# The zeros ahead of the experts' regions, written during the tenth unit of attention

## The chip, the cores and the metric

The kernel runs on one core of one Trainium2 chip. The metric is the time of the device for one execution, in microseconds (us); the median of the runs is compared.

## What is computed

Three stages follow each other. Attention is computed for 8 batches, 8 heads, 576 positions and 32 memory slots. Its output, 4608 rows of 512 columns, goes through a mixture of 8 experts in which each row uses one expert, and then through a feed-forward network with a hidden width of 2048.

```python
def reference(**kwargs):
    ...
    attn_out = _attn_ref(**attn_kwargs)
    x = np.ascontiguousarray(attn_out.transpose(0, 2, 1, 3)).reshape(B * S, H * D)
    x = _moe_ref(x=x, **moe_kwargs)       # e = argmax of logits; out = gate * relu(x w1[e]) w2[e]
    return _moe2_ref(x=x, **moe2_kwargs)  # softplus(x w_in) w_out
```

## The kernel before

**Attention and routing** (`attention_and_routing`). The 4608 rows are 18 units (`u`) of two tiles of 128 rows. A unit goes through `scores` (matmuls, then maximum, exponential and sum, down to the weights `an`), `transp` (TensorE turns `an`, ScalarE copies it to `aT`), `values` (the matmuls `px`, copied to `xrow`, and the logits `lg`), `route` (the expert of each row) and `rank` (the place of each row in its expert's region). Units 0 to 15 are routed in pairs, the last two alone. `rank` ends with indirect DMAs on GpSimd's queue that write the rows into the DRAM buffer `xs`, which has one region for each expert: 512 rows ahead of it (`PAD`) and then room for 4608 rows. The rows ahead of a region are read when a slot is not full, so they have to hold zeros. `pad` writes them for one expert from the tile `zero`, a transfer of 1056 KB on SyncE's queue; there are eight.

**The first slot.** After unit 10 (`CHOICE`) the counts so far are known. `choose(0, ...)` picks the expert with most rows and a start row into `few` (columns 0 to 2, `pick[0]`). `fetch` makes SyncE load the two values into registers (L468, L469), read 256 rows of `xs` into `raw0` (L51), and load that expert's weights: four tiles of `w1` (buffers `k`) and four of `w2` (buffers `j`), 512 KB each (L102), with the gates `ig0` between them (L473). `chosen` is this slot's computation, spread over the last units by `STEPS`: VectorE turns `raw0` into `xt` (L486), 32 matmuls in full precision make the hidden rows `ph` (L491; the profile counts 64, since each is two instructions), ScalarE and VectorE make `h` from them (L125, L126) and split the tiles of `w2` in two parts (L58, L61), and 48 matmuls make `py` (L67 to L69).

**The second choice** follows the last `rank`: `choose(1, ...)` writes `pick[1]` (L455 to L464). VectorE then builds the table of all further slots (`listed`, L601 to L643).

**The further slots** (`experts`). SyncE loads the start row of the second choice (`head(1, SP, ...)`, L746, a TENSOR_LOAD of `few`) and reads two quarters of 512 rows of `xs` into `raw`; ScalarE's queue reads the other two quarters. VectorE turns `raw` into `xt` (L675), ScalarE and VectorE split it to `hl`, and TensorE starts the slot with the matmuls `ph<-hl,k` (L67 to L69). From there the slots follow each other without a wait, and the last network after them.

**What sets the order.** Every engine runs its instructions in the order of the built program, SyncE its transfers too: an instruction that waits holds all that stand behind it on its engine. In the attention part a planner makes that order: it places an instruction by the time at which it holds its inputs to be ready, so that code written later can stand earlier. A transfer that reads `xs` at a register's row is taken to depend on all writes to `xs` that the code has ahead of it. `once` takes a write out of this against the groups in `apart`: after `fetch` the writes to `xs` are declared apart from its reads ("full"), ahead of it they are not.

Of the kernel before, what the change touches and what calls it, by code (L numbers as in the profile page):

```python
# [25 lines left out]
E, F = 8, 1024  # L26
# [10 lines left out]
TAB = TABU + MAXS  # L37
STEPS = {14: 4, 15: 2, 16: 2, 17: 1}
CHOICE = 10
PADS = range(11, 15)  # L40
PAD = UNIT
RG = PAD + NT
ROW = 528
# [28 lines left out]
def pad(eng, xs, zero, e):  # L72

    return eng.dma_start(xs[e * RG:e * RG + PAD].rearrange("(p a) c -> p a c", p=P),
                         zero.unsqueeze(1).to_broadcast([P, PAD // P, ROW]))
# [101 lines left out]
def attention_and_routing(tc, env):  # L177
    nc = tc.nc
    V, A, G, PE, SP = nc.vector, nc.scalar, nc.gpsimd, nc.tensor, nc.sync
    qT, kv, phi, mid, wg, mbias, w1, w2 = (env[n] for n in ("qT", "kv", "phi", "mid", "wg", "mbias", "w1", "w2"))  # L180
    xs, table, nslots, pick, ig0, ps_y, K, Q, J = (
        env[n] for n in ("xs", "table", "nslots", "pick", "ig0", "ps_y", "K", "Q", "J"))

    with ExitStack() as st:
# [37 lines left out]
        zero = c.tile([P, ROW], F32, name="zero")  # L222
# [20 lines left out]
        def load(b):  # L243
            p0 = 9 * (b // 2)
            lo, hi = (0, 5) if b % 2 == 0 else (5, 9)
            o = b % 2 * 64
            phs[b] = pht[b % 3]
            SP.dma_start(phs[b][:, :, o:o + S], phi[:, b * S:(b + 1) * S].rearrange("(g p) s -> p g s", p=P))
            for t in range(p0 + lo, p0 + hi):
                SP.dma_start(kvt[t % 12], kv[t * P:(t + 1) * P])  # L250
            qs[b] = qst[b % 3]
            SP.dma_start(qs[b], qT[:, b * S:(b + 1) * S].rearrange("(g p) s -> p g s", p=P))
# [97 lines left out]
        def scores(u):  # L350
            ps = ps_s.tile([P, 2, H * M], F32, name="ps", tag="s")
            for k in range(2):
                for p in range(4):
                    for hf in range(2):
                        n = 4 * u + 2 * k + hf
                        b, o = n // 9, (n % 9) * 64
                        PE.matmul(ps[64 * hf:64 * hf + 64, k, 64 * p:64 * p + 64],
                                  qs[b][:, p, o:o + 64],
                                  kvT[b][:, p // 2, 0, 64 * (p % 2):64 * (p % 2) + 64],
                                  start=True, stop=True)  # L360
            s3 = ps.rearrange("p k (h m) -> p (k h) m", m=M)
            mx = sm.tile([P, 2 * H], F32, name="smx", tag="smx")
            V.tensor_reduce(mx, s3, axis=AX, op=ALU.max)
            sc = wk.tile([P, 2 * H, M], F32, name="sc", tag="sc", bufs=3)
            V.tensor_tensor(sc, s3, mx.unsqueeze(2).to_broadcast([P, 2 * H, M]), ALU.subtract)
            A.activation(sc, sc, AF.Exp, scale=0.125)
            ss = sm.tile([P, 2 * H], F32, name="ss", tag="ss")
            V.tensor_reduce(ss, sc, axis=AX, op=ALU.add)
            V.tensor_scalar(ss, ss, 1e-9, None, op0=ALU.add)
            V.reciprocal(ss, ss)  # L370
            an = wk.tile([P, 2 * H, M], F32, name="an", tag="an", bufs=3)
            for k in range(2):
                hs = slice(k * H, (k + 1) * H)
                (V if u >= UNITS - LATE else G).tensor_tensor(an[:, hs], sc[:, hs], ss[:, hs].unsqueeze(2).to_broadcast([P, H, M]), ALU.mult)
            at[u] = an

        def transp(u):
            an = at[u].rearrange("p (j h) m -> p j (h m)", j=4)
            pt = ps_t.tile([P, 4, P], F32, name="pat", tag="t")
            for j in range(4):  # L380
                PE.transpose(pt[:, j, :], an[:, j, :], ident)
            aT = wk.tile([P, 4, P], F32, name="aT", tag="aT", bufs=3)
            A.activation(aT, pt, AF.Copy)
            at[u] = aT

        def values(u, k):
            aT = at[u]
            gi = group[u]
            if u == units[gi][0] and k == 0:
                logit[gi] = sm.tile([P, 2 * len(units[gi]), E], F32, name="lg", tag="lg")  # L390
            lg, xr = logit[gi], xrow[gi % 3]
            W = 2 * D + E
            px = ps_y.tile([P, 2, 512], F32, name="px", tag="y")
            t = 2 * u + k
            halves = [(0, P)] if 2 * t // 9 == (2 * t + 1) // 9 else [(0, 64), (64, 64)]
            for g in range(2):
                for o, n in halves:
                    b = (2 * t + o // 64) // 9
                    for r in (0, 1):
                        PE.matmul(px[o:o + n, r, g * W:(g + 1) * W],  # L400
                                  aT[64 * r:64 * r + 64, 2 * k + g, o:o + n],
                                  vz[b][64 * r:64 * r + 64, g, 2 * D:], start=True, stop=True)
            i = 2 * (u - units[gi][0]) + k
            pw = px[:, :, 0:2 * W].rearrange("p r (g c) -> p r g c", g=2)
            A.activation(xr[:, i, 0:DM].rearrange("p (g r c) -> p r g c", g=2, r=2), pw[:, :, :, 0:2 * D], AF.Copy)
            V.tensor_reduce(lg[:, i, :], pw[:, :, :, 2 * D:].rearrange("p r g e -> p e r g"),
                            axis=mybir.AxisListType.XY, op=ALU.add)
# [44 lines left out]
        def choose(i, rows):  # L452

            n, d, m = cnt
            V.tensor_tensor(n, rows, past[i], ALU.subtract)  # L455
            V.tensor_reduce(most[:, 0:1], n, axis=AX, op=ALU.max)
            V.scalar_tensor_tensor(d, n, most[:, 0:1], desc[0:1], op0=ALU.is_equal, op1=ALU.mult)
            V.tensor_reduce(most[:, 1:2], d, axis=AX, op=ALU.max)
            V.tensor_scalar(pick[i][:, 0:1], most[:, 1:2], -1.0, float(E), op0=ALU.mult, op1=ALU.add)
            V.scalar_tensor_tensor(m, d, most[:, 1:2], past[i], op0=ALU.is_equal, op1=ALU.mult)  # L460
            with nc.allow_low_precision(reason="whole numbers below 2**24"):
                V.tensor_reduce(pick[i][:, 1:2], m, axis=AX, op=ALU.max)
            V.tensor_scalar(d, d, most[:, 1:2], float(UNIT if i else SLOT), op0=ALU.is_equal, op1=ALU.mult)
            V.tensor_tensor(past[i + 1], past[i], d, ALU.add)  # L464

        def fetch():
            W.tiles()
            x0 = SP.value_load(pick[0][:, 1:2], min_val=0, max_val=E * RG - SLOT)  # L468
            e = SP.value_load(pick[0][:, 0:1], min_val=0, max_val=E - 1)  # L469
            read = rows_in(nc, SP, raw0, xs[ds(x0, SLOT)], SLOT)  # L470
            for i in range(4):
                W.load(0, i, e)
            read.append(SP.dma_start(ig0, xs[ds(x0, SLOT), DM:DM + 2].rearrange("(t p) c -> p t c", p=P)))  # L473
            full(tc, *read)
            apart.append("full")
            for i in range(4):
                W.load(1, i, e)
# [23 lines left out]
        def once(w):  # L501

            for group in apart:
                tc.declare_no_dep(w.ins, group=group, reason="disjoint rows")
            tc.add_to_no_dep_group("xs", w.ins)
            return w
# [27 lines left out]
        def point(i):  # L534
            if i in points:
                f, b = points[i]
                f(b)
# [15 lines left out]
        for u in range(UNITS):  # L553
            if u == 0:
                load(2)
            point(4 * u)
            if u + 2 < UNITS:
                scores(u + 2)
            if u in (0, 2, 5, 7, 9):
                load(3 + (0, 2, 5, 7, 9).index(u))  # L560
            point(4 * u + 1)
            values(u, 0)
            point(4 * u + 2)
            if u + 1 < UNITS:
                transp(u + 1)
            values(u, 1)
            if u and u - 1 == units[group[u - 1]][-1]:
                rank(group[u - 1])
                if u == CHOICE:
                    choose(0, base[(group[u - 1] + 1) % 2][0:1])  # L570
                    fetch()
            if u == units[group[u]][-1]:
                route(group[u])
            point(4 * u + 3)
            if u == CHOICE:
                steps = chosen()
            if u in PADS:
                for e in range(2 * (u - PADS[0]), 2 * (u - PADS[0]) + 2):
                    once(pad(SP, xs, zero, e))
            for i in range(STEPS.get(u, 0)):  # L580
                next(steps)
        rank(len(units) - 1)
# [410 lines left out]
```

## Time and profile before

| | us |
|---|---|
| median of 3 runs | 1412.92 |
| lowest and highest of them | 1411.44, 1417.55 |
| profiled execution, time of the device | 1422.22 |
| profiled execution, span | 1420.2 |

The span runs from the first instruction to the last. Of its 1420.2 us TensorE (PE) is busy in 1370.2. Attention, routing and the first slot take the first 182 us, the further slots go on to about 609 us, and the last network ends the span. Times in the rows below are counted from the start of the span. The granted clock of TensorE is given as a share of 2.4 GHz: 0.50 is 1.2 GHz. A duration of a matmul in the profile includes its way through the array, so matmuls that follow each other overlap: 16 of L491 stand in 3.70 us, though each lasts 0.38.

### The profile page before, as it was taken

The page shows a single profiled execution, that of the slowest core. Times are in us where ns is not written, and L with a number is a line of the kernel's source. Part 1 is how long each engine was busy: PE and PEld are TensorE (multiplying, and loading weights), DVE is VectorE, ACT ScalarE, POOL GpSimd, SP SyncE. Part 2 cuts the span into 40 slices and gives each one's busy share as a digit, 9 for nine tenths or more (in the row PEclk, how much of TensorE's full clock was granted, in tenths as well). Part 3 has the DMA queues.
Part 4 walks back from the last instruction along what each step waited for, and adds up shares of the span by engine and source line. Part 5 has one row for each costly group of instructions (what it writes and reads, how often), then busy time and mean ns, then how long its engine had stood idle before and what let it go on. Part 6 is the DMA issues. An engine that isn't in the chain of part 4 may idle for free.

```text
span 1420.2 us, 19794 instructions
## 1 busy us (share of the span) xinstructions
PE 1370.2 (96%) x7312; PEld 1100.9 (78%) x7312; DVE 922.5 (65%) x1699; ACT 674.6 (48%) x1193; POOL 256.9 (18%) x267
## 2 busy tenths in 40 slices
PE   7997989999999999889999999999999999999997
PEld 5775758878888888668888888888888888888885
DVE  4665857777877775769665756657566575665553
ACT  3554435444443445356544545445454454544443
POOL 1343314333434334300100101001010010100101
PEclk8889989999999999999999999999999999999998
DMA  9975984445334566244010200202001020000000
GB/s 357 402 285 202 374 240 102 104 113 140 95 99 127 170 213 182 89 143 133 23 38 0 60 1 23 38 0 60 1 23 38 0 60 1 23 8 1 30 1 30
DMA packets 94338, 143.03 MB, mean 101 GB/s; under 512 B 16160, under 2 KB 54048, under 8 KB 94240
## 3 DMA queue, kind: packets, MB, share of 16 engines
q1 hardware_dynamic: 86320, 120.94, 28.5%
q0 software_dynamic: 5760, 19.17, 3.5%
q10 hardware_dynamic: 2160, 1.63, 0.4%
q8 instruction: 58, 0.95, 0.3%
q14 instruction: 40, 0.33, 0.1%
HBM read 122.28 MB, written 44.62 MB: 118 GB/s over the span
## 4 chain that ended last, share of the span: by engine, by line
PE 50%; issue 6%; POOL 0%; DMA 0%; ACT 0%; DVE 0%; POOLq 0%; SPq 0%
PE po L67 8%; PE po L69 8%; PE po L68 8%; PE ph L67 8%; PE ph L69 8%; PE ph L68 8%; POOL out L928 0%; DMA s<-wsc 0%; POOLq L989 0%; ACT u L908 0%; DVE g L914 0%; DVE c L913 0%; ACT u L909 0%; ACT g L910 0%; ACT k L58 0%
## 5 line engine op out<-in xcount | busy, mean ns | idle before, releaser
L67 PE MATMUL ph<-hl,k 128*128 128x512 f32 (+1 forms) x536 | 204.3, 381 | 8.2 <-ACT hl L58 5.4
L68 PE MATMUL ph<-hl,k 128*128 128x512 f32 (+1 forms) x536 | 204.3, 381 | 0.0
L58 ACT ACTIVATE gh<-g 128x512 fp32r<-128x512 f32 x144 | 91.0, 632 | 228.3 <-DVE g L915 228.0
L912 DVE TENSOR_SCALAR c<-u 128x512 f32<-128x512 f32 x144 | 61.5, 427 | 194.7 <-ACT u L909 185.2
L928 POOL DMA_INDIRECT out<-ob,ids x36 | 41.3, 1147 | 767.9 <-ACT ob L927 661.7
L69 PE MATMUL ph<-hl,k 128*128 128x512 f32 (+1 forms) x456 | 173.1, 380 | 0.0
L61 DVE TENSOR_TENSOR gl<-g,gh 128x512 fp32r<-128x512 f32 x144 | 99.2, 689 | 84.7 <-ACT gh L58 83.7
L908 ACT ACTIVATE u<-ph 128x512 f32<-128x512 f32 x144 | 86.1, 598 | 133.0 <-PE ph L69 128.1
L67 PE MATMUL py<-q,h 128*128 128x512 f32 x304 | 121.7, 400 | 6.9 <-ACT h L125 5.9
L67 PEld LDWEIGHTS ph<-hl,k 128*128 128x128 f32 x536 | 101.6, 190 | 31.4 <-ACT hl L58 8.2
L69 PE MATMUL py<-q,h 128*128 128x512 f32 x304 | 120.7, 397 | 0.8 <-DVE h L126 0.8
L68 PEld LDWEIGHTS ph<-hl,k 128*128 128x128 f32 x536 | 101.6, 190 | 21.3 <-DVE hl L61 1.8
L126 DVE SCALAR_TENSOR_TENSOR h<-ph,h 128x512 fp32r<-128x512 f32 (+1 forms) x88 | 54.2, 616 | 82.6 <-ACT h L125 82.4
L913 DVE TENSOR_TENSOR c<-c,u 128x512 f32<-128x512 f32 x144 | 99.6, 692 | 4.5
L915 DVE TENSOR_TENSOR g<-g,c 128x512 f32<-128x512 f32 x144 | 99.0, 688 | 4.2
L914 DVE SCALAR_TENSOR_TENSOR g<-ph,g 128x512 f32<-128x512 f32 x144 | 98.3, 684 | 0.9 <-ACT g L910 0.9
L69 PEld LDWEIGHTS ph<-hl,k 128*128 128x128 f32 x456 | 85.7, 188 | 16.3
L125 ACT ACTIVATE h<-ph 128x512 fp32r<-128x512 f32 (+1 forms) x88 | 47.3, 537 | 107.4 <-PE ph L69 101.1
L909 ACT ACTIVATE u<-u 128x512 f32<-128x512 f32 x144 | 90.8, 631 | 4.0
L910 ACT ACTIVATE g<-u 128x512 f32<-128x512 f32 x144 | 90.8, 631 | 3.9
L67 PE MATMUL po<-k,gh 128*128 128x512 f32 x216 | 85.9, 398 | 0.0
L69 PE MATMUL po<-k,gl 128*128 128x512 f32 x216 | 85.5, 396 | 0.0
(236 smaller groups left out, 3083.7 us busy)
## 6 DMA issues: line engine op xcount, KB each, us to landing
k<-w SPq DMA_DIRECT2D x43, 512.0 KB
j<-w SPq DMA_DIRECT2D x43, 512.0 KB
k<-kv SPq DMA_DIRECT2D x36, 512.0 KB
d<-wffn SPq DMA_DIRECT2D x32, 512.0 KB
q<-qT SPq DMA_DIRECT2D x8, 1152.0 KB
raw<-ys SPq DMA_DIRECT2D x36, 256.0 KB
xs<-zero SPq DMA_DIRECT2D x8, 1056.0 KB
ys<-y SPq DMA_DIRECT2D x8, 1026.0 KB
```

Of the source, the lines that this page charges most:

```text
L58: hi_eng.activation(hi, x, AF.Copy)
L61: lo_eng.tensor_tensor(lo, x, hi.bitcast(F32), ALU.subtract)
L67: nc.tensor.matmul(out, lh, rh, start=start, stop=False)
L68: nc.tensor.matmul(out, lh, rl, start=False, stop=False)
L69: nc.tensor.matmul(out, ll, rh, start=False, stop=stop)
L908: A.activation(u, ph, AF.Abs)
L909: A.activation(u, u, AF.Exp, scale=-1.0)
L910: A.activation(g, u, AF.Ln, bias=1.0)
L912: V.tensor_scalar(c, u, 1.0, 1.0, op0=ALU.add, op1=ALU.subtract)
L913: V.tensor_tensor(c, c, u, ALU.subtract)
L914: V.scalar_tensor_tensor(g, ph, 0.0, g, op0=ALU.max, op1=ALU.add)
L915: V.tensor_tensor(g, g, c, ALU.subtract)
```

## The change

The eight transfers of zeros were written in pairs after units 11 to 14; now all eight are written in unit 9, ahead of `choose(0, ...)` and `fetch`, which come in unit 10. In the code they stand behind the loads of the last batch (`load` of unit 9).

```diff
-PADS = range(11, 15)
+PADS = 9
...
             if u in (0, 2, 5, 7, 9):
                 load(3 + (0, 2, 5, 7, 9).index(u))
+            if u == PADS:
+                for e in range(E):
+                    once(pad(SP, xs, zero, e))
             point(4 * u + 1)
...
-            if u in PADS:
-                for e in range(2 * (u - PADS[0]), 2 * (u - PADS[0]) + 2):
-                    once(pad(SP, xs, zero, e))
```

Below, a row is a line of the code, an operation, what it writes and reads, and how often it stands there. `few` holds both choices, `raw_182` is `raw0`.

SyncE, from the last load of attention (`q`) to the first read of the first slot, as a difference:

```order
 L252 DMA q_174<-qT 128x4x576
+L74 DMA xs<-zero 512x1x528 x8
 L468 TENSOR_LOAD few
 L468 ISA x2
 L469 TENSOR_LOAD few
 L469 ISA x2
+L746 TENSOR_LOAD few
+L746 ISA x2
 L51 ISA
 L51 DMA raw_182<-xs 32x8x128
```

The zeros moved ahead of the first choice's values, as written; the load of the second choice's start row (L746), which stood behind the whole first slot and the zeros, now stands ahead of the first slot's read. It waits for VectorE's L462 of `choose(1, ...)`; before, too, but there the first slot's transfers were ahead of it.

TensorE, the end of routing (`pr`) and what follows it, now:

```order
L432 MATMUL pr<-ohb,ones_b 128x8
L491 MATMUL ph<-xt,k_1749 128x256 x8
L491 MATMUL ph<-xt,k_1750 128x256 x8
L67 MATMUL py<-q_1746,h 128x512
L68 MATMUL py<-q_1748,h 128x512
L69 MATMUL py<-q_1746,h 128x512
L67 MATMUL py<-q_1746,h 128x512
L491 MATMUL ph<-xt,k_1751 128x256 x8
L68 MATMUL py<-q_1748,h 128x512
L491 MATMUL ph<-xt,k_1752 128x256 x8
L69 MATMUL py<-q_1746,h 128x512
```

Before, these 32 matmuls of L491 stood in seven pieces between the matmuls of units 14 to 17 and the last two `pr`; all of them now stand behind the last `pr`.

VectorE, from the end of the table (`listed`), now:

```order
L642 TENSOR_SCALAR few<-sums_3_2522 1x1
L643 TENSOR_SCALAR few<-few 1x1
L486 STREAM_TRANSPOSE xt<-raw_182 128x256 x4
L126 SCALAR_TENSOR_TENSOR h<-ph,h 128x256 x2
L61 TENSOR_TENSOR q_1748<-j_1753,q_1746 128x512 x2
```

The four transposes of `raw0`, and the work on `h` and on the parts of `w2`, moved from between the instructions of the last units to behind the table.

ScalarE, the relus of the first slot and its two quarters of the next slot's rows, now:

```order
L125 ACTIVATE h<-ph 128x256
L746 TENSOR_LOAD few
L746 ISA x2
L51 ISA
L51 DMA raw<-xs 32x16x128
L125 ACTIVATE h<-ph 128x256 x2
L51 ISA
L51 DMA raw<-xs 32x16x128
```

Before, both transfers stood together behind the eighth and last relu (L125) of the first slot; now one stands behind the sixth, and the other still behind the eighth. The relus moved with L491 behind routing.

## Rows read from the trace of the kernel before

**Rows 1.** The page: busy time of the engines, and the chain that ended last.

```profile
PE 1370.2 (96%) x7312; PEld 1100.9 (78%) x7312; DVE 922.5 (65%) x1699; ACT 674.6 (48%) x1193; POOL 256.9 (18%) x267
...
PE 50%; issue 6%; POOL 0%; DMA 0%; ACT 0%; DVE 0%; POOLq 0%; SPq 0%
```

**Rows 2.** Windows: stretch, length; PE, PEld, DVE, ACT, POOL busy; granted clock; DMA share; GB/s.

```profile
141.30:169.40 28.10, 25.53 (x202) 19.27 (x203) 22.75 (x112) 14.45 (x32) 10.84 (x11) 0.94 1.05 387
...
187.20:197.50 10.30, 10.11 (x18) 5.43 (x19) 5.86 (x9) 4.14 (x8) 1.05 (x1) 0.50 1.07 344
197.50:207.50 10.00, 10.00 (x44) 8.19 (x43) 6.71 (x8) 4.35 (x9) 3.44 (x4) 0.99 0.78 204
...
280.00:290.00 10.00, 10.00 (x45) 8.04 (x43) 9.25 (x15) 5.83 (x12) 2.14 (x2) 1.00 0.17 52
```

**Rows 3.** The waits of SyncE's queue from 95 to 260 us: total, times, longest.

```profile
SPq L746 <- DVE past L464: 16.7, 1, 16.7
...
SPq L51 <- DMA xs<-xrow,ri: 10.2, 2, 7.1
```

**Rows 4.** Timeline of SyncE's queue: start, duration, line, transfer, count.

```profile
99.19 0.38 SPq L252 DMA_DIRECT2D q<-qT  x1
124.84 1.92 SPq L51 DMA_DIRECT2D raw<-xs  x4
...
132.60 20.69 SPq L74 DMA_DIRECT2D xs<-zero  x8
...
178.22 0.90 SPq L51 DMA_DIRECT2D raw<-xs  x2
```

**Rows 5.** Timeline of VectorE; in brackets the idle time ahead, and what ended it.

```profile
153.98 0.76 DVE L374 TENSOR_TENSOR an<-sc,ss 128x256 f32<-128x256 f32 x2
...
169.22 0.15 DVE L462 TENSOR_REDUCE few<-cnt 1x1 int32<-1x8 f32 x1
...
177.60 0.14 DVE L643 TENSOR_SCALAR few<-few 1x1 int32<-1x1 int32 x1
...
185.74 0.71 DVE L675 STREAM_TRANSPOSE xt<-raw 128x512 f32<-128x512 f32 x1 [4.55 <-DMA raw<-xs]
...
187.76 0.70 DVE L675 STREAM_TRANSPOSE xt<-raw 128x512 f32<-128x512 f32 x1
```

**Rows 6.** Timeline of TensorE around the first slot and the start of the next.

```profile
155.68 1.56 PE L491 MATMUL ph<-xt,k 128*128 128x256 f32 x6
...
157.44 2.40 PE L491 MATMUL ph<-xt,k 128*128 128x256 f32 x10
...
161.19 3.70 PE L491 MATMUL ph<-xt,k 128*128 128x256 f32 x16
166.62 0.70 PE L491 MATMUL ph<-xt,k 128*128 128x256 f32 x2 [1.73 <-DVE h L126]
...
170.20 0.58 PE L67 MATMUL py<-q,h 128*128 128x512 f32 x1
...
187.17 0.80 PE L67 MATMUL ph<-hl,k 128*128 128x512 f32 x1 [5.42 <-ACT hl L58]
```

**Rows 7.** Groups of instructions from 141.3 to 169.4 us: count, busy us, mean ns.

```profile
L491 PE MATMUL ph<-xt,k 128*128 128x256 f32 x60 | 15.4, 399 | 1.7 <-DVE h L126 1.7
```

**Rows 8.** Windows as in rows 2, of 2 and 10 us, for DMA and the clock.

```profile
60.00:70.00 10.00, 9.15 (x92) 7.36 (x94) 5.94 (x29) 4.79 (x11) 2.63 (x5) 0.56 1.04 407
70.00:80.00 10.00, 10.00 (x126) 7.21 (x126) 4.47 (x19) 3.85 (x8) 5.20 (x7) 0.59 0.75 282
...
112.00:114.00 2.00, 2.00 (x41) 1.44 (x34) 1.05 (x6) 0.18 (x1) 1.19 (x2) 0.89 0.00 0
...
122.00:124.00 2.00, 0.00 (x0) 0.00 (x0) 0.01 (x1) 0.18 (x1) 0.98 (x1) 1.00 0.59 224
...
126.00:128.00 2.00, 2.00 (x34) 1.49 (x33) 1.97 (x9) 0.15 (x1) 0.00 (x0) 0.52 0.95 214
...
130.00:132.00 2.00, 2.00 (x30) 1.53 (x22) 1.39 (x7) 0.77 (x2) 0.00 (x0) 1.00 1.06 379
```

## The prediction

> **What bounds the kernel now.** The busy times and the chain come first [rows 1]: TensorE is busy in 96% of the span and the chain that ended last is TensorE's, so a microsecond counts only if TensorE loses or gains it. The windows then show where it loses any [rows 2]. It waits 5.4 us up to 187.17 [rows 6], and from there to 197.5 it runs at a granted clock of 0.50 (1.2 GHz) and brings off 18 matmuls; from 197.5 on it does 44 in 10 us, and the windows of 10 us from there to 290 are all full. So whatever moves the 19th matmul of the further slots, at 197.5, moves the end by as much: behind it lies no wait in which a delay could be lost. The wait of 5.42 us is for `hl`, that for `raw` [rows 5, 6], and `raw` was issued at 178.22, when the last scattered rows had landed, for which SyncE waited 7.1 us [rows 3, 4].
>
> Then SyncE's queue. It issues nothing between 99.6 and 124.84, when the first choice is known and the first slot's rows are read, and issues the zeros from 132.60 to 153.3 [rows 4]. After that it waits 16.7 us for the second choice, which VectorE writes at 169.37 [rows 3, 5]. The first slot's matmuls of L491, 64 in the trace, run in the meantime: 60 of them stand between 141.3 and 169.4, beside the last units [rows 7].
>
> **The zeros themselves.** Eight transfers of 1056 KB are 8.65 MB, at 387 GB/s [rows 2] 22.3 us of all DMA engines. Before, they share the DMA engines with weights and scatters, at shares of 1.05 to 1.06 from 130 to 169 [rows 2, 8]. Now they are issued from 99.6 on [rows 4], behind the last batch's transfers, which are through before 112 (from 112 to 114 the DMA engines carry nothing [rows 8]). So they end between 122 and 134, in time that was largely free. That they leave 132 to 153 brings nothing by itself: what TensorE does there was not waiting for a transfer. What it may cost the units under way is a rival below.
>
> **The wait that is added.** On SyncE the load of the second choice's start row (L746) now stands ahead of the first slot's read. It waits for the second choice, and behind it are queued the read of `raw0`, the eight weight tiles, the gates and then `raw`. So the first slot is not begun at 124.84 but after the end of routing. That the zeros have to have landed before `raw0` is read is then without effect: they are down over 20 us earlier. On TensorE all 64 matmuls of L491 (in the order: 32) stand behind the last `pr`, on VectorE the transposes stand behind the table. Four terms follow; T is the time at which VectorE has written the second choice, 169.37 before.
>
> *T.* Routing ends earlier, since the first slot's work no longer stands between. One L491 takes 3.70 / 16 = 0.231 us [rows 6]. From the last unit's `an` at 153.98 to 169.37 [rows 5] pass 15.4 us; 34 of the 64 (6, 10, 16 and 2) stand there ahead of the last `pr`, 7.9 us, with a wait of 1.73 us that only they have [rows 6], together 9.6 us. Part of it ran while VectorE worked, so I take 7.5. From 141.3 to 154 stand 16 more, 3.7 us, of which I take 3; the last ten of the 60 come behind that `pr`. T moves forward by 10.5, to 158.9. The bounds: 5 us, if VectorE's own chain sets the pace; 13.3 us, if all 50 and the wait were on the path.
>
> *From T to the first L491.* SyncE was through with L746 at 178.22 - 7.1 = 171.1, 1.7 us after the choice [rows 3 to 5]. The rows land about 4 us later if it goes as with the windows after 124.84 (0.5 MB at 214 GB/s and the way there) [rows 4, 8], and at most 7.5 us later, as `raw` did (178.22 to 185.74) [rows 4, 5]. VectorE meanwhile builds the table: 169.37 to 177.74 is 8.4 us, with two L126 of the first slot in between [rows 5]; without them I take 7.6. So the table and the rows are ready at about T + 8, and with the first transpose L491 starts at T + 8.5 (8.2 to 9.7).
>
> *The first slot.* 64 x 0.231 = 14.8 us at full clock, and the 48 matmuls of `py` stand from 170.20 to the wait of 5.42 us ahead of 187.17, 11.5 us, of which the last one's end is 0.2: 11.2 us [rows 6]. TensorE has then waited about 10 us, twice as long as the 5.42 after which it ran at half clock for 10.3 us [rows 2, 6]. I charge the same: half of 10.3, 5.1 us. Shorter and longer stretches stand in the trace: less than 4 us from 126 (0.52) to 130 (1.00), and 17 us of the twenty from 60 (0.56 and 0.59) [rows 8]; 2 to 8.5 us are the ends. Sum: 31.1 us, so `py` ends at T + 39.6.
>
> The Trainium skill, page "TensorE: Matmul & The Clock Gate", part 1, says that activity releases a throttle that is the default, and that the number of slow matmuls varies from run to run (6, 11 or 14 in one kernel). With 14 slow ones the charge would be an estimated 14 x 0.23 = 3.2 us in place of 5.1, and the time 1418; the trace's 18 slow ones from 187.2 to 197.5 speak for the larger charge.
>
> *The start of the further slots.* The last quarter of `raw` is issued by ScalarE behind the eighth relu, at about T + 30.3, and lands 4 to 7.5 us later. The first `hl` follows 1.4 us behind the transpose's start, and the further three every 2.0 us [rows 5], so the fourth is there at T + 42 to T + 46, when TensorE wants it at T + 41.7. I take a wait of 1.5 us (0 to 4). What is regained is the half clock: 18 matmuls in 10 / 44 x 18 = 4.1 us and not in 10.3 [rows 2]. The 19th matmul then comes at T + 39.6 + 1.5 + 4.1 = T + 45.2.
>
> **The sum.** 158.9 + 45.2 = 204.1, against 197.5 before: 6.6 us later. Equality would need T = 152.3. The profiled execution took 1422.2 and would take 1428.8; the median of the runs shown is 9.3 lower, and with the same difference it goes from 1412.9 to 1419.5, which I round to 1420. With the good ends (T = 156.1, 2 us for the clock, no wait for `hl`) it is 0.8 earlier, 1412; with T = 164.4 and 4 us for `hl` it is 14.6 later, 1427.5.
>
> **The rivals.** *A larger regain.* Before, TensorE loses 5.4 us ahead of 187.17 and 6.2 at half clock, 11.6 us in all; the change removes both, because `raw` now travels under `py`. Against it stand the 10 us after T and the half clock there. If routing ends at 156 and the clock comes back in 4 us, as at 130, the result is 1412 to 1416. For it: the short stretch is there in the rows. Against: the only wait of that length was followed by the long one. To end on the other side, faster by over 0.5%, T would have to be 145 or less, ahead of the last unit's `an` at 154 even now; it decides from T = 152.3.
>
> *The zeros slow the units.* From 100 to 130 they fill the DMA engines beside units 9 to 12. In that stretch TensorE already stands still from 122 to 124 (0.00 busy) [rows 8], and the rows do not say for what. If two such stops are added, 4 to 5 us, the result is 1424 or 1425. Against it: from 60 to 70 the DMA engines were as full (1.04) and TensorE was busy 9.15 of 10 us [rows 8].
>
> *Routing does not get faster.* If the latency from engine to engine, and not the first slot's work, sets the pace of the last units, T stays near 169 and the sum is 17 us: 1430. For it: VectorE is busy only 22.75 of 28.1 us there [rows 2]. Against: 60 matmuls of L491 take half of that stretch on TensorE, in order with the `px` and `pr` [rows 7].
>
> *The change does not do what it says*, that is, L746 does not hold the first slot: then `raw0` would be read at about 128, and with the zeros out of the way of the scatters the 7.1 us of SyncE and the wait of TensorE for `raw` would go, 1406 to 1408. The order of SyncE speaks against it outright.
>
> **How the numbers follow.** The forecast (1416 to 1424) has 0.50, the larger regain 0.19, slowed units 0.12, unchanged routing 0.12, and 0.07 are for the last rival or a result on the far side. About 0.5%, 7.1 us, is what a measurement of this kernel can tell from no change, so the border to slower is 1420, and the forecast lies on it: half of its chance is "same". Same: 0.25 + 0.19 + 0.02 = 0.46; slower: 0.25 + 0.12 + 0.12 = 0.49; faster: 0.05. The range from 1412 to 1430 leaves out the far sides of the first and the last cases, some 0.2.
>
> **What would show it.** The profile after should show the zeros issued from about 99.6 on; SyncE waiting at L746 until about 159, and the read of `raw0` right behind it; TensorE idle for about 10 us from about 157; L491 in one piece from about 167, slow at first; `py` running into `ph` with almost no wait; and the full clock at that start. It is wrong if `raw0` is read before routing ends, if T lies before 153 or after 166, or if TensorE waits anew behind the 19th matmul.

## The result, and the profile after it

The changed kernel takes 1419.75 us (median of 12 runs, 1415.73 to 1424.25), the kernel before 1412.57 us (12 runs beside it, 1409.60 to 1417.55). The ratio is 1.0052, with a 95% interval of 1.0037 to 1.0066. So it is slower by about half a per cent. A second timing on another chip gave 1.0040 [1.0024, 1.0057], against 1414.19 us. The forecast was 1420, with 1412 to 1430 as its range. The time came as forecast; the terms that gave it did not, and most of this part is about them.

The profiled execution after took 1424.25 us, the longest of the twelve, with a span of 1422.5. Busy time of the page, the line that answers [rows 1]:

```profile
PE 1366.4 (96%) x7312; PEld 1100.4 (77%) x7312; DVE 927.6 (65%) x1699; ACT 675.1 (47%) x1193; POOL 255.9 (18%) x267
```

The windows that answer [rows 2], and one of the first 6 us of the first slot (columns as there: busy time of PE, PEld, DVE, ACT, POOL, granted clock, DMA share, GB/s):

```profile
141.30:169.40 28.10, 13.94 (x66) 11.54 (x65) 19.34 (x102) 6.25 (x15) 7.84 (x8) 0.63 0.88 275
157.00:163.00 6.00, 5.91 (x16) 4.85 (x17) 0.42 (x1) 0.38 (x1) 0.00 (x0) 0.58 1.04 413
188.70:199.00 10.30, 9.88 (x18) 5.36 (x19) 5.86 (x9) 4.11 (x8) 1.01 (x1) 0.53 0.37 81
280.00:290.00 10.00, 10.00 (x45) 8.12 (x44) 9.22 (x15) 4.86 (x9) 2.98 (x2) 1.00 0.18 52
```

TensorE's busy time from 141.3 to 169.4 has halved against [rows 2] (25.53 before), and the stretch of 18 matmuls at the lower clock is still there, now from 188.7 to 199. What SyncE waits for and what it issues, which answers [rows 3, 4]:

```profile
SPq L746 <- DVE cnt L463: 24.7, 1, 24.7
```

```profile
96.72 23.24 SPq L74 DMA_DIRECT2D xs<-zero  x8
147.77 2.33 SPq L51 DMA_DIRECT2D raw<-xs  x4
...
160.29 1.75 SPq L51 DMA_DIRECT2D raw<-xs  x2
```

The zeros run from 96.72 to 119.96, and SyncE then stands 24.7 us at L746, ahead of the first slot's read (four quarters at 147.77). The second slot's rows are four quarters as well. SyncE reads two at 160.29, ScalarE the other two, behind two of its ReLUs:

```profile
172.21 0.38 ACTq L51 DMA_DIRECT2D raw<-xs  x1
...
174.91 0.37 ACTq L51 DMA_DIRECT2D raw<-xs  x1
```

VectorE and TensorE, which answer [rows 5, 6]:

```profile
146.58 0.15 DVE L462 TENSOR_REDUCE few<-cnt 1x1 int32<-1x8 f32 x1
...
187.28 0.71 DVE L675 STREAM_TRANSPOSE xt<-raw 128x512 f32<-128x512 f32 x1 [9.99 <-DMA raw<-xs]
```

```profile
157.09 9.57 PE L491 MATMUL ph<-xt,k 128*128 128x256 f32 x32 [12.09 <-DMA k<-w]
...
167.44 3.61 PE L491 MATMUL ph<-xt,k 128*128 128x256 f32 x16
...
188.71 0.50 PE L67 MATMUL ph<-hl,k 128*128 128x512 f32 x1 [3.94 <-ACT hl L58]
...
199.04 0.63 PE L67 MATMUL ph<-hl,k 128*128 128x512 f32 x1
```

The second choice is written at 146.73. TensorE idles for 12.1 us behind the last `pr` (14.1 us with the 1.97 it waits ahead of that `pr`) and does the first slot from 157.09 to 184.8. It then waits 3.94 us for rows that have landed at 187.28, 12 us after ScalarE's last read, and brings off the 19th matmul of the further slots at 199.04. From there to the end 1223.5 us pass, and 1222.7 after the 19th matmul at 197.51 in the first profile of before. So the difference between these two lies ahead of that matmul, as the prediction says.

### The profile page after: what moved, and what is told of

Read it like the earlier page. It is cut to its first block, busy times and chain, and to the rows that moved or that the text cites. A ratio compares the mean times of both kernels' runs of the same rounds, so it can differ in the third digit from the quotient of the medians.

```text
span 1422.5 us, 19801 instructions
## 1 busy us (share of the span) xinstructions
PE 1366.4 (96%) x7312; PEld 1100.4 (77%) x7312; DVE 927.6 (65%) x1699; ACT 675.1 (47%) x1193; POOL 255.9 (18%) x267
## 4 chain that ended last, share of the span: by engine, by line
PE 50%; issue 6%; POOL 0%; DMA 0%; ACT 0%; DVE 0%; POOLq 0%; SPq 0%
PE po L67 8%; PE po L69 8%; PE po L68 8%; PE ph L67 8%; PE ph L69 8%; PE ph L68 8%; POOL out L928 0%; DMA s<-wsc 0%; POOLq L989 0%; DVE g L914 0%; ACT u L908 0%; DVE c L913 0%; ACT u L909 0%; ACT g L910 0%; ACT k L58 0%
## 5 line engine op out<-in xcount | busy, mean ns | idle before, releaser
L125 ACT ACTIVATE h<-ph 128x512 fp32r<-128x512 f32 (+1 forms) x88 | 47.3, 538 | 124.2 <-PE ph L69 101.1
```

## The experiments

**A second look at before**, with nothing edited.

> The kernel before, once more, for a second profile of it. The first profile of before has four stretches in which all engines stand still (58 to 61, 106 to 109, 122 to 124 and 139 to 141 us, some 11 us together) and was 9.7 us above the median of before. If these belong to one execution and not to the kernel, the second choice is written near 158 us here and no longer at 169.4, the first matmul of the first slot starts near 145, and the run takes 1410 to 1414 us. If they belong to the kernel, the same stops stand there again and the choice is written within 2 us of 169.4.

It took 1417.6 us (span 1415.5), on a chip where the median of before was 1414.84. Waits and issues of SyncE, and then VectorE and TensorE, in this second profile of before:

```profile
SPq L51 <- DMA xs<-xrow,ri: 12.6, 3, 9.1
...
SPq L51 <- DMA xs<-zero: 8.7, 4, 3.0
```

```profile
127.47 24.98 SPq L74 DMA_DIRECT2D xs<-zero  x8
172.26 0.90 SPq L51 DMA_DIRECT2D raw<-xs  x2
```

```profile
152.09 0.15 DVE L462 TENSOR_REDUCE few<-cnt 1x1 int32<-1x8 f32 x1
...
179.60 0.71 DVE L675 STREAM_TRANSPOSE xt<-raw 128x512 f32<-128x512 f32 x1 [4.38 <-DMA raw<-xs]
```

```profile
130.73 0.70 PE L491 MATMUL ph<-xt,k 128*128 128x256 f32 x2
...
150.15 3.27 PE L491 MATMUL ph<-xt,k 128*128 128x256 f32 x14
...
181.03 0.79 PE L67 MATMUL ph<-hl,k 128*128 128x512 f32 x1 [16.41 <-DMA j<-w]
...
190.42 0.39 PE L67 MATMUL ph<-hl,k 128*128 128x512 f32 x1
```

None of the stops is there; they belonged to the one execution from which the prediction was made. I call this one the quiet profile of before. The second choice is written at 152.24, not at 169.37. That is earlier than expected (158), and the total came 3.6 us above what I expected. The reading of before changes with it. The first slot is through near 164, and TensorE then waits 16.41 us. The row names a weight tile, the last to come by the profile; what was late is `raw`. Its read goes out at 172.26, 20.0 us behind the choice, because SyncE waits there 9.5 us for scatters (two of the three waits in the row) and 8.7 us for the zeros themselves, which all land late in a stretch where zeros, weights and scatters share the DMA engines (a DMA share of 0.97 to 1.04 from 150 to 170 us). In the first profile it went out 8.85 us behind the choice [rows 4, 5]. So before has room between routing and `raw`. Counted from the first choice (written at 119.75 in the first profile, at 113.03 here) the second choice comes 49.6 and 39.2 us later, and yet the 19th matmul 77.8 and 77.4. From the one profile to the other the choice moved by 17.1 us, the 19th matmul by 7.1 (190.42 to 197.51) and the span by 4.7.

**A second look at the changed kernel.**

> The changed kernel once more, for a second profile. If what I read in its first profile belongs to the kernel, the second choice is written at 146 to 148 us, the first matmul of the first slot starts at 156 to 158, TensorE waits 3 to 5 us for raw near 184 to 189, and the clock is at half in the 10 us after it. If that was one execution's accident, the wait or the low clock behind it is missing.

This came on a chip on which before itself took 1422.99 us; the run took 1436.43. Rows of VectorE and TensorE:

```profile
106.30 0.69 DVE L363 TENSOR_REDUCE smx<-ps 128x16 f32<-128x512 f32 x1 [3.56 <-remote]
...
159.82 0.15 DVE L462 TENSOR_REDUCE few<-cnt 1x1 int32<-1x8 f32 x1
```

```profile
172.81 10.15 PE L491 MATMUL ph<-xt,k 128*128 128x256 f32 x32 [14.56 <-DVE xt L486]
...
200.91 0.39 PE L67 MATMUL ph<-hl,k 128*128 128x512 f32 x1
```

The stops are there now, and here they pass through nearly whole. The choice comes 13.2 us later than in the first profile after, the 19th matmul 11.1 later (210.12) and the span is 12.2 longer. The idle time ahead of the first slot stands at 14.56 us. The wait ahead of the further slots is gone, which I had not expected, and yet the 18 matmuls take 9.2 us, at a granted clock of 0.81:

```profile
201.00:210.00 9.00, 6.98 (x19) 4.00 (x18) 4.56 (x8) 3.62 (x7) 0.53 (x1) 0.81 0.61 168
```

Before, at 0.56, they took 9.4 (181.03 to 190.42), and after, at 0.53, 10.3. So most of that time is not the clock. `hl` comes a tile every 2.01 us, and TensorE follows it.

**The zeros elsewhere, with the first slot not held.** Three places were tried: one unit earlier on SyncE; on GpSimd's queue; on ScalarE's queue in the tenth unit.

```
-PADS = 9
+PADS = 8
```
```
-                    once(pad(SP, xs, zero, e))
+                    once(pad(G, xs, zero, e))
```
```
-                    once(pad(SP, xs, zero, e))
+                    once(tc.keep_in_program_order(pad(A, xs, zero, e)))
```

> The change, with one number different: the zeros are written in the ninth unit, one unit earlier. In the planned order SyncE then reads the first slot ahead of its wait for the second choice again, and the first slot's matmuls lie among the last units and the routing, as before the change, while the zeros are still early. Theory (the time is lost to SyncE's wait, which holds the first slot behind the second choice): faster than before by the part of the routing that comes forward and with nothing held, 1402 to 1410 us, and the 3.9 us wait for raw and the half clock behind it are gone or shorter. Rival (the time is lost to the zeros' traffic beside the units): the traffic is the same and lies ahead of a load of keys besides, so it stays as slow as the changed kernel or slower, 1418 to 1424 us.

> The change, with the zeros issued from GpSimd's queue in place of SyncE's, where they stand ahead of the first units' normalisations and so run tens of us earlier, beside the first units. The first slot is read ahead of the wait for the second choice, as before the change. Theory (the wait is what costs): 1402 to 1410 us, unless the first units wait on GpSimd for the issues. Rival (the traffic costs wherever it lies beside units): 1417 to 1424 us.

> The change, with the zeros issued from ScalarE's queue, pinned in the tenth unit (near 101 us), so that they lie in the same quiet stretch of the DMA engines as in the changed kernel; SyncE reads the first slot ahead of its wait for the second choice, and the first slot's matmuls lie among the last units and the routing, as before the change. What I read from the second profile of before (second choice written at 152.2, first slot ended near 164, but SyncE's read of raw issued only at 172.3, behind scatters that landed late in a stretch in which zeros, weights and scatters fill the DMA engines) gives the theory: where the zeros lie is a gain, what holds the first slot is the loss. It expects raw to be read within 9 us of the second choice, near 160 to 163, the further slots' first matmul near 170 in place of 181, and 1400 to 1406 us. The rival (zeros beside the units cost what the change costs, the hold is free) expects 1416 to 1422 us.

Measured: 1.0062 [1.0044, 1.0079], 1.0016 [0.9998, 1.0035] and 1.0094 [1.0080, 1.0109]. None was faster; the theory's numbers were missed three times, and the rival's were met once (1423.32 us, one unit earlier). The traces say that none of the three is the clean case that I wanted. One unit earlier, the zeros stand ahead of the last batch's keys on SyncE's queue, and the units starve (a window of the version with the zeros in the ninth unit):

```profile
114.00:140.00 26.00, 16.27 (x214) 11.55 (x212) 11.81 (x53) 9.27 (x20) 1.96 (x2) 0.77 1.01 319
```

TensorE is busy in 16.27 of these 26 us, in the quiet profile of before in 24.91. On GpSimd's queue the zeros run beside the first units, whose loads fill the DMA engines anyway; in the profiled execution, the longest of ten (1422.81 us), the first choice comes at 131.8 in place of 113.0. On ScalarE's queue ScalarE itself stands still while it issues them:

```profile
101.69 15.83 ACTq L74 DMA_DIRECT2D xs<-zero  x7
117.62 0.60 ACT L405 ACTIVATE xrow<-px 128x512 f32<-128x512 f32 x1 [15.64 <-DMA xs<-zero]
```

The Trainium skill, page "DMA: Bandwidth & Descriptors", section "Issuing engines are not separate DMA queues", calls the time that a sequencer needs to initiate a transfer usually small against the transfer. On SyncE and ScalarE it is not here: eight of 1056 KB hold SyncE for 23.24 us, and seven hold ScalarE for 15.83. On GpSimd's queue it is: six of the same transfers are issued in 4.70 us and two in 1.46. SyncE has nothing else to do in that stretch; on ScalarE the units wait.

The profile of the run on GpSimd's queue shows something else. Its second choice is 18.6 us later than in the quiet profile of before, and its span only 5.6 us longer. Late routing costs this arrangement far less than it is late.

**The hold alone.** The zeros stay on GpSimd's queue, and the fetch of the first slot is written behind the second choice, with all the steps of its computation.

```
                     choose(0, base[(group[u - 1] + 1) % 2][0:1])
-                    fetch()
+                    apart.append("full")
...
         choose(1, base[len(units) % 2][0:1])
+        fetch()
+        steps = chosen()
```

> The same as the run with the zeros on GpSimd's queue, with the fetch of the first slot written behind the second choice, so that SyncE waits for that choice before it reads the first slot, and TensorE has the first slot's matmuls behind the routing, as in the changed kernel; the zeros lie where they lie in the run without this. Theory (the wait is what costs): 8 to 14 us slower than the run without it, at 1414 to 1422 us. Rival (the traffic costs, the wait is free): within 2 us of the run without it.

1436.46 us, ratio 1.0168 [1.0142, 1.0193]; without the hold 1415.18, so 21.3 us, more than the 8 to 14 expected. First the choice and SyncE's read of `raw` without the hold, then the choice and TensorE with it:

```profile
170.72 0.15 DVE L462 TENSOR_REDUCE few<-cnt 1x1 int32<-1x8 f32 x1
```

```profile
179.47 0.90 SPq L51 DMA_DIRECT2D raw<-xs  x2
```

```profile
154.04 0.15 DVE L462 TENSOR_REDUCE few<-cnt 1x1 int32<-1x8 f32 x1
```

```profile
168.81 9.20 PE L490 MATMUL ph<-xt,k 128*128 128x256 f32 x32 [16.34 <-DMA k<-w]
...
200.57 0.79 PE L67 MATMUL ph<-hl,k 128*128 128x512 f32 x1 [4.45 <-ACT hl L58]
```

With the hold the choice is 16.7 us earlier, and the 19th matmul 12.8 later (210.73 against 197.94). But these absolute times are not the hold's alone. The two executions differ ahead of anything that the hold moves, here from 60 to 80 us, without the hold and then with it:

```profile
60.00:80.00 20.00, 20.00 (x209) 15.28 (x208) 9.71 (x38) 8.94 (x19) 5.18 (x6) 0.54 1.04 400
```

```profile
60.00:80.00 20.00, 18.98 (x324) 14.77 (x320) 16.95 (x68) 12.53 (x27) 7.85 (x10) 1.00 1.03 403
```

At a granted clock of 0.54 TensorE does 209 matmuls there, at 1.00 it does 324, and the first choice comes at 131.77 and 121.60. Counted from it, the second choice comes 6.5 us earlier with the hold (32.6 for 39.1) and the 19th matmul 23.0 us later (89.1 for 66.2), near the 21.3 us of the medians. This is the cleanest pair: the zeros are issued at the same times in both (4.6 to 9.3 and 40 to 42 us), and holding the first slot behind routing costs more than routing gains by it. How much is not the changed kernel's figure: here the first slot's read waits for the scatters as well (6.1 us) and goes out 7.2 us behind the choice, in the changed kernel 1.0.

**What in the hold costs.** In the first of these runs the reads of the first slot are declared free of the zeros, so that SyncE issues them early; the order on VectorE and TensorE stays. In the second, SyncE reads all four quarters of `raw`.

```
+            for r in read:
+                tc.declare_no_dep(r.ins, group="zeros", reason="disjoint rows")
             full(tc, *read)
```
```
-            for x, eng, js in ((x0, SP, (0, 1)), (xa, A, (2, 3))):
+            for x, eng, js in ((x0, SP, (0, 1, 2, 3)),):
```

> The changed kernel, with the first slot's reads declared free of the zeros, so that SyncE reads the first slot and its weights ahead of its wait for the second choice, as before the change; the order on VectorE and TensorE stays that of the changed kernel (the first slot's transposes behind the table of slots, its matmuls behind the routing), and ScalarE's reads of raw stay behind its ReLUs. If SyncE's wait alone is what costs: raw and weights land early, TensorE starts the first slot near 145, 1405 to 1411 us. If it is the place of the first slot on VectorE and TensorE: TensorE still starts it at 156 to 157, behind the transposes, and the time is 1415 to 1420 us.

> The changed kernel, with all four quarters of the second slot's rows (raw) read from SyncE's queue; in the changed kernel ScalarE reads two of them, behind the first slot's sixth and eighth ReLU, at 172.2 and 174.9, and they land at 187.3, 3.9 us after TensorE ran out of work. Theory (those two reads, and the low clock of the 18 matmuls after the wait, are the last link of the loss): raw lands before TensorE ends the first slot at 184.6, the wait of 3.9 us is gone and the 18 matmuls take 4 to 5 us in place of 10.3, so 8 to 11 us faster than the changed kernel, 1409 to 1412 us. Rival (TensorE waits there for something else, or the clock falls all the same): 1417 to 1421 us.

Both ran on the chip of the second look at the changed kernel (before 1422.99, the one run of the changed kernel 1436.43). The first gave 1436.26, 1.0090 [1.0074, 1.0107], which that one run can't tell from no change. The rows are read at 130.64, ahead of the choice, and TensorE still idles 13.76 us until VectorE's transposes, which stand behind the table:

```profile
130.64 2.71 SPq L51 DMA_DIRECT2D raw<-xs  x4
```

```profile
174.51 9.89 PE L493 MATMUL ph<-xt,k 128*128 128x256 f32 x32 [13.76 <-DVE xt L488]
```

L491 starts 12.0 us behind the choice (162.47), in the changed kernel's three profiles 9.8 to 12.8. So SyncE's wait is not the only thing that holds the first slot: its place on VectorE and TensorE does so without that wait. Why the planner keeps that place when the reads no longer depend on the zeros, no run shows.

The second gave 1432.82, 1.0058 [1.0040, 1.0076], 3.6 us less than the changed kernel's one run there; 8 to 11 were expected. In its profile the start of the further slots looks as forecast:

```profile
198.01 0.71 DVE L675 STREAM_TRANSPOSE xt<-raw 128x512 f32<-128x512 f32 x1 [0.17 <-issue]
...
206.61 0.39 PE L69 MATMUL py<-q,h 128*128 128x512 f32 x1
206.84 0.40 PE L67 MATMUL ph<-hl,k 128*128 128x512 f32 x1
...
210.96 0.39 PE L67 MATMUL ph<-hl,k 128*128 128x512 f32 x1
```

`raw` is transposed from 198.01 on, under `py`; TensorE runs from `py` into `ph` with no wait, and the 18 matmuls take 4.1 us. From the first L491 to the 19th matmul it is 30.86 us, against 37.31 in the second profile of the changed kernel and 41.95 in the first: 6.4 or 11.1 us. How much of that stays in the whole is not shown: the median stands against a single run, and the profiled execution itself took 1437.73 us, the longest of its six and longer than that run.

**Both advantages together.** As in the run with the reads declared free, and besides, VectorE's instructions from the 16th unit on are queued behind the first slot's transposes, and TensorE's from the 18th on behind its matmuls. The second version moves both one or two units back.

```
+BEHIND = (0, 15), (1, 17)
...
+            with ExitStack() as held:
+                for ins in behind(u):
+                    held.enter_context(tc.issue_after(ins.ins))
```
```
-BEHIND = (0, 15), (1, 17)
+BEHIND = (0, 17), (1, 18)
```

> The changed kernel's zeros (SyncE's queue, tenth unit), with the first slot back where it was before the change: its reads are declared free of the zeros, so that SyncE reads it ahead of its wait for the second choice, and from the unit after the transposes on, VectorE's and TensorE's later instructions are queued behind the first slot's transposes and matmuls. Theory (the zeros' new place is a gain of some 10 us, the first slot's new place a loss of more): the second slot's rows are read within 10 us of the second choice, TensorE has the first slot done by then, the wait ahead of the further slots is some us shorter than before, and the ratio to before is 0.990 to 0.997. Rival (zeros in the tenth unit cost by themselves, or the read of the first slot behind the zeros is late enough to undo the gain): 1.003 to 1.008.

> The changed kernel, timed beside the others of this call. Its ratio to before was 1.0052 in the first result. The one run of it on the chip of the last call stood at 1.0094 of a before that was itself 0.6% slower there; both profiles on that chip show stretches in which all engines stand still. Theory (before has slack between the second choice and the end of the scatters, which takes up such stops, and the changed kernel has none): the ratio follows the chip, 1.004 to 1.006 where before takes 1412 to 1416 us and 1.007 to 1.010 where it takes over 1420. If the stops cost both alike: 1.004 to 1.006 on either.

The first version takes 1411.93 us, 0.9987 [0.9973, 1.0002] of before, on the chip on which the changed kernel takes 1418.55, 1.0040 [1.0024, 1.0057]. The intervals do not touch, so it is faster than the changed kernel, by 6.6 us in the medians. Against before it is 2.3 us, which can't be told from nothing, and less than I expected. A likely reason why it is no more stands on VectorE:

```profile
137.48 1.42 DVE L490 STREAM_TRANSPOSE xt<-raw 128x256 f32<-128x256 f32 x4 [6.35 <-DMA raw<-xs]
138.82 0.65 DVE L364 TENSOR_REDUCE smx<-ps 128x16 f32<-128x512 f32 x1
...
158.44 0.15 DVE L463 TENSOR_REDUCE few<-cnt 1x1 int32<-1x8 f32 x1
```

```profile
167.30 0.90 SPq L52 DMA_DIRECT2D raw<-xs  x2
```

```profile
175.80 0.80 PE L68 MATMUL ph<-hl,k 128*128 128x512 f32 x1 [4.50 <-ACT hl L59]
...
185.28 0.39 PE L68 MATMUL ph<-hl,k 128*128 128x512 f32 x1
```

The first slot's rows are read behind the zeros and land at 137.5. VectorE waits for them 6.35 us with the last unit's scores queued behind, and the second choice comes at 158.59. But `raw` is now read 8.7 us behind the choice, not 20.0, and the 19th matmul comes 26.7 us behind it, not 38.2. Not all of these 11.5 us come from the zeros' place: in the first profile of before, with the zeros where they were and a late choice, the way was 28.1. From the first choice to the 19th matmul it is 74.6 us, against 77.4 and 77.8 before, so some 3 us are gained in this profile, near the 2.3 of the medians.

The line for the second timing of the changed kernel: the ratio on a chip where before takes 1414 is 1.0040. On the other chip I have one run of it, at 1.0094, so that stops cost the changed kernel more is likely from the profiles and not shown by timings.

> The run before the last three's best (zeros early, first slot free), with the first slot's transposes two units later on VectorE: there VectorE stood 6.4 us at them for the slot's rows (137.5 us), with the last unit's scores queued behind (138.8 in place of some 129), so the second choice came at 158.6 and no earlier than before the change. With the transposes behind the last unit's scores and the first group of the routing they meet rows that have landed. Theory (the second choice then comes near 150 to 153, and the second slot's rows are read 8.5 us later): the 19th matmul of the further slots some 8 us earlier than in that run, near 177, and a ratio to before of 0.991 to 0.995. Rival (the first slot's matmuls, now later too, set the end, or the rows of the second slot land no earlier): 0.997 to 1.001.

1427.77 us, 1.0024 [1.0010, 1.0038], on a chip with stops (before 1425.02): the rival's side, and worse. The transposes no longer wait, but the choice comes at 174.47, 28 us behind the last unit's scores at 146.18; in the first profile after it is 14.1 us (132.62 to 146.73). TensorE does the last `pr` at 170.49, behind 40 of the first slot's 64 L491, though its input was written at 158.98, and VectorE takes the first slot's ReLU halves between the steps of routing. It waits for one of them 4.56 us, but that wait holds another stop: the relu on ScalarE has its releaser given as remote, and from 162.7 to 164.2 TensorE, VectorE and ScalarE all stand still.

```profile
164.21 0.38 ACT L126 ACTIVATE h<-ph 128x256 fp32r<-128x256 f32 x1 [4.60 <-remote]
```

So this run does not settle what the wait of 6.35 us costs. No version here beats before for certain.

**TensorE kept busy.** The changed kernel, with 48 matmuls of nothing behind the last `pr`.

```
+            if gi == len(units) - 1:
+                with tc.issue_after(done.ins):
+                    w = ps_t.tile([P, 4, P], F32, name="warm", tag="t")
+                    for i in range(48):
+                        PE.matmul(w.rearrange("p k c -> p (k c)"), ones_b, lead, start=True, stop=True)
```

> The changed kernel with 48 more matmuls of nothing (128x512 in bf16, on a tile that nobody reads) behind the last matmul of the routing, where TensorE of the changed kernel is idle for 14 us, so that the first slot's matmuls need not start at half the clock. If the half clock ahead of the first slot costs what I took for it (5.1 us): the first 32 matmuls of the slot take 7 to 8 us in place of 9.6 to 10.2, the whole is 2 to 6 us faster than the changed kernel. If the clock is not what sets that stretch: within 1 us of the changed kernel. If the extra matmuls reach past the transposes: slower by what they reach.

1418.81 us, 1.0049 [1.0029, 1.0070], 0.3 us from the changed kernel beside it. TensorE around the first slot, at the start of the next, and at 611:

```profile
144.72 12.02 PE L439 MATMUL warm<-lead,ones_b 128*128 128x512 bf16 x47 [0.24 <-issue]
156.57 8.82 PE L496 MATMUL ph<-xt,k 128*128 128x256 f32 x40
...
184.05 0.50 PE L67 MATMUL ph<-hl,k 128*128 128x512 f32 x1 [2.27 <-ACT hl L58]
...
611.09 0.80 PE L68 MATMUL ph<-hl,first 128*128 128x512 f32 x1 [5.45 <-DMA s<-wsc]
```

The first slot starts at full clock (a granted clock of 1.00 from 156.5 to 162, 0.22 us each; after, it was 0.58 from 157 to 163), and `py` ends 25.2 us after the first L491 in place of 27.7 and 26.9 in two profiles without them. Its 19th matmul comes at 193.54, 47.3 us behind the second choice in place of 52.3 and 50.2, and 5.5 us earlier than in the first profile after. Of these 5.5 us 3.3 went at 611, where TensorE waits 5.45 us for a transfer and 2.1 in that profile. So the slow start of the first slot costs 1.7 to 2.5 us there, and in the medians nothing came of them; whether the loss at 611 is of every execution I don't know.

## Why the prediction was right, and where only in its sum

**The mechanism held in the main.** The first slot follows the second choice, TensorE idles between, and the 19th matmul moves back. The pair on GpSimd's queue shows that a hold costs by itself. What holds is only in part what the prediction put first: it counted from SyncE's wait at L746, and the run with SyncE's read set free shows that the order on VectorE and TensorE, which the prediction names beside it, is enough. With that order put back as well, the time fell by 6.6 us. Whether L746 alone would hold the first slot was not tried. Two rivals fell: the zeros do not slow the units where the change puts them (the last unit's scores come at 132.62, against 134.25 in the quiet profile of before), and routing does get faster.

**The terms** (us; the last column is the profile taken with the second timing):

| step | predicted | after | second timing |
|---|---|---|---|
| T, second choice written | 158.9 | 146.7 | 142.7 |
| T to the first L491 | 8.5 | 10.4 | 9.8 |
| first L491 to the end of `py` | 31.1 | 27.7 | 26.9 |
| wait ahead of the further slots | 1.5 | 3.9 | 3.2 |
| 18 matmuls | 4.1 | 10.3 | 10.3 |
| 19th matmul, behind T | 45.2 | 52.3 | 50.2 |

*T* lies outside its bounds (156.1 to 164.4) and ahead of 153, which the prediction had named as a sign of being wrong. What was off most is the starting point: 169.37 belongs to one execution with stops, and the quiet profile has 152.24. Against that T moves forward by 5.5 us (counted from the first choice 5.3, and 6.0 in the second timing), and the 10.5 taken was nearly twice that. The lower bound, 5 us, was the better value; that VectorE's own chain sets the pace, which the prediction gives as its reason, was not tested.

*From T to the first L491* the table alone took 8.5 us, for which 7.6 was taken, and L491 then waited for the first slot's weights (the 12.09 us of the row end with a `k` tile), for which the sum has no term.

*The first slot* was charged 5.1 us for a slow start. The first 32 matmuls took 9.57 and 8.78 us, where 32 x 0.231 is 7.4, so it is 1.4 to 2.2 (2.8 in the second look, with 10.15). The Trainium skill's page "TensorE: Matmul & The Clock Gate", part 1, with its 14 slow matmuls, gave an estimated 3.2 and was nearer than my row, though still high.

*The start of the further slots* is the step that failed. I took the 10.3 us of [rows 2, 6] for the price of the half clock and counted its return as a gain of 6.2. They are mostly the pace of `hl`: at a clock of 0.81 it was 9.2. That stretch shrinks to 4.1 only if `raw` has been transposed ahead of time, as where SyncE reads all of it. I put its last quarter at T + 30.3, landing 4 to 7.5 us later; it went out at T + 28.2 and landed 12 us later, beside the next expert's weights.

*What made the sum come out.* The prediction has -10.5 for T and +17.1 for the way from T to the 19th matmul (45.2 against 28.1), +6.6 in all. Against the quiet profile of before it is -5.5 and +14.1 (52.3 against 38.2), +8.6, and 7.0 in the spans. Both terms were too large by 5.0 and 3.0, and they have opposite signs. The way in before was longer than I took it, 38.2 for 28.1, because in that profile `raw` is held by scatters and zeros until 20.0 us behind the choice, and not 8.85. By the second timing's profile, counted from the first choice, the two terms are -6.0 and +12.0. That the median came within 0.3 us of 1420 is luck. So the rival that the prediction put down as a result on the far side had something to it: in the profiles the zeros out of the way of scatters and `raw` are a gain, and the hold takes it back and more; in a median the gain is not shown.

The other rivals: no large regain came, since the lower clock at the start of the further slots stayed (0.53), and the first slot is held.

*"Behind it lies no wait in which a delay could be lost"* holds for the windows shown, up to 290; between 500 and 620 us there are waits of up to 2.8 us in the profiles before and after, and one of 5.45 in the run with more matmuls.

**What stays open:** what the stops are; how much of the loss each of the late quarters of `raw` and the idle 14 us carries in the median; why the planner leaves the first slot behind routing when its reads are free; and whether the arrangement with both advantages can be had without VectorE waiting in it.

## What to carry to other kernels

Moving large writes into a quiet stretch of the DMA engines pays by what the transfer that waits behind them gains, so look for that transfer first (here `raw`, behind scatters and the zeros themselves). When a planner sets the order, moving a write ahead of a read can put that read's whole chain behind other work, on engines that never touch the write, and here it did so even with the reads declared free of it; compare the order on every engine. And take a second profile before a term is read from an absolute time: between two profiles of before the choice stood 17 us apart and the end 5. Times counted from an event shortly ahead of the stretch in question (here the first choice) agree better between executions: 77.8 and 77.4 us to the 19th matmul in those two.

## What was not expected of the hardware

In some executions TensorE, VectorE and ScalarE stand still together several times, for 2 to 4 us each, the last one seen at 164 us, with the releaser given as remote, while the DMA engines and GpSimd carry on. The window from 104 to 106 us of the run with the first slot moved back the furthest:

```profile
104.00:106.00 2.00, 0.00 (x0) 0.00 (x0) 0.06 (x1) 0.00 (x1) 2.00 (x3) 1.00 1.05 397
```

Before took 1422.99 and 1425.02 us on the two chips whose profiles showed them, and 1414 to 1415 on the two whose profiles did not. The profile that the prediction rests on had them, though the median beside it was 1412.9, so that they belong to the chip is not shown. Issuing eight transfers of 1056 KB keeps SyncE for 19.9 to 25.0 us, which is near the 22.3 us estimated for their bytes at 387 GB/s; on GpSimd's queue the same eight are issued in 6.2 us. The granted clock of one stretch differs between executions of the same kernel: from 60 to 80 us it was 0.67 and 0.91 in the two profiles of the changed kernel that show no stops, with the first choice at 112.82 and 109.41.
